# The first queries of an attention kernel loaded ahead of the values and transposed among the warm-up matmuls

## The chip, the cores and the metric

The kernel runs on one core of one Trainium2 chip. The metric is the device time of one execution in microseconds, the median of 13 runs: 168.59 us (168.45 to 169.01). A profile is one such execution, recorded by the hardware.

## The reference

Two stages follow each other. The first is attention in blocks with a learned sorting of the key and value blocks; the second is a maxout layer of two matmuls.

```python
for _ in range(5):                                  # P: 4 x 8 matrices of 8 x 8
    P = P - np.max(P, axis=-1, keepdims=True)
    P = np.exp(P)
    P = P / (np.sum(P, axis=-1, keepdims=True) + 1e-09)
    P = P / (np.sum(P, axis=-2, keepdims=True) + 1e-09)
k_sorted = np.einsum('bhij,bhjcd->bhicd', P, k_b)   # blocks of 96 tokens
v_sorted = np.einsum('bhij,bhjcd->bhicd', P, v_b)
scores = scale * np.matmul(q_b, k_sb.transpose(0, 1, 2, 4, 3))
attn = softmax(scores)                              # over the 96 tokens of the block
x = np.matmul(attn, v_sb)                           # then (3072 tokens, 512)
out = np.maximum(x @ w1, x @ w2) @ w_out            # 512 -> 1024 -> 512
```

There are 4 items (batch), 8 heads, 768 tokens, head size 64. All inputs come as float32 and are cast to bf16 while they are loaded.

## The kernel before, in words

The order of all instructions is written out by hand; no scheduler moves them. Each engine takes its own instructions in that order and waits on semaphores where it needs another engine's result. TensorE computes, ScalarE and VectorE bring results from PSUM to SBUF, GpSimd (POOL) issues all loads and SyncE (SP) the stores. PSUM is one ring of four buffers of 4 KB per partition (L62, tag `ps`): every product stage takes the next buffer, and waits until the last reader of that buffer is done.

The head of the kernel prepares the first item:

- POOL issues the loads in the order values 0 (three pieces, `load_v`, L169), the identity matrix, keys 0 (three pieces, L160), queries 0 (four pieces, one for each pair of heads, L143), then the expert weights (L189, L182). A later DMA that uses the semaphore of an earlier one waits until that one has landed.
- `sinkhorn` (L241) runs five times on the 32 x 64 tile `p_sb`: an exp on ScalarE (L242), then six short steps on VectorE (L248 to L255). The last writes `p_bf`. After the first two come mask steps on VectorE, after the third `selections`.
- `turn_v` (L219) reorders the values in SBUF. ScalarE does 18 columns after each of the third and the fourth sinkhorn step's VectorE part has been issued, and 20 and 24 after the fifth; VectorE does the last 16 of 96 after the masks. The turns stand between the exps in ScalarE's queue.
- `keep_streaming` (L77) multiplies zeros, so that TensorE is kept busy: 86 matmuls of 142 columns first, then two groups of six of 512 columns, each of which waits for a small VectorE fill that stands in the fourth and the fifth sinkhorn step (`late_zeros`, L85).
- `block_diagonals` (L317 to L335) makes from `p_bf` the two 128 x 64 matrices that sort keys and values.
- `sort_k` (L408, three groups) and `sort_v` (L429, four groups) follow, each evicted with a cast by the engine that the call names ("A" ScalarE, "D" VectorE). `q_transposes` (L383) turns one half of the queries, 24 transposes into one PSUM buffer, and evicts with one VectorE copy of 128 x 1536. The first half stands between the second and the third `sort_v`, the second half after the first two score groups.
- Scores (L498, exp L506), values (L525; reciprocal and product by VectorE, L536 and L542), transposes of x (L563) and the first expert products (L627) then alternate in a written order. Query half 0 serves head pairs 0 and 1, half 1 pairs 2 and 3; scores 2 need half 1. The x transposition 0 needs values 0 and 1, transposition 1 needs values 2 and 3; expert products (0, 2) need the first, (1, 3) the second.

After the head a loop over the four items issues expert and output products, and between them the attention steps of the next item (`first_tail` and so on). There `pick` gives an eviction to ScalarE or VectorE by counts of their load, which every earlier eviction has changed.

## Time and profile before

| | us |
|---|---|
| median of 13 runs | 168.59 |
| the profiled execution | 168.59 |
| its span, first to last instruction | 166.8 |
| TensorE matmul busy | 160.1 |
| ScalarE busy | 83.1 |
| VectorE busy | 79.3 |
| first product on `p_bf` starts | 11.53 |
| first key product starts | 12.71 |
| expert products (1, 3) start | 25.81 |

Times inside the span count from its start. A line of the timeline gives start, length, engine, line, operation, output and inputs, shape, count, and in brackets how long the engine stood idle before it and what ended that. A count over one merges neighbours of the same kind. A matmul line's length includes the drain of its last matmul, so it overlaps the line after it. The chain of waits goes back from the last instruction to whatever released it; its lines give start, length and what.

### The profile page before, as it was taken

The numbers are of one execution on the slowest core, as the hardware profiler recorded it, in microseconds if no ns is written. First come the engines' busy times: TensorE is split into PE (matmuls) and PEld (weight loads), VectorE is DVE, ScalarE is ACT, GpSimd is POOL, SyncE is SP. The second block draws the span as 40 slices with busy tenths as digits, with TensorE's granted clock in tenths as the row PEclk, the third lists the DMA queues.
The fourth block names the chain that finished last, engine by engine and source line by source line (L and its number), as shares of the span: only waits on it lengthen the run. The fifth ranks groups of instructions, "written<-read, shape, count | busy, mean of one in ns | idle before, by whom it ended". The sixth has DMA issues, their size and how long they took to land.

```text
span 166.8 us, 4555 instructions
## 1 busy us (share of the span) xinstructions
PE 160.1 (96%) x2011; PEld 96.7 (58%) x2011; DVE 79.3 (48%) x182; ACT 83.1 (50%) x101; POOL 29.6 (18%) x46
## 2 busy tenths in 40 slices
PE   7999899999999999999999999999999999999991
PEld 7948676766545555557655554575655545654451
DVE  5878885847483784535257874080642420000011
ACT  3587868674168627045752253467447206642010
POOL 7956586231022000000004120000000000000000
PEclk9999999999999999999999999999999999999999
DMA  3999999999999993659403999988025253000342
GB/s 54 191 203 196 198 207 206 212 201 216 212 210 210 216 230 77 173 111 199 106 0 61 148 232 182 188 223 110 2 51 173 47 177 126 0 0 0 126 154 103
DMA packets 30404, 23.90 MB, mean 143 GB/s; under 512 B 16752, under 2 KB 25200, under 8 KB 30384
## 3 DMA queue, kind: packets, MB, share of 16 engines
q0 software_dynamic: 11040, 13.37, 47.7%
q1 hardware_dynamic: 19200, 10.17, 25.9%
q8 instruction: 16, 0.26, 0.6%
q10 hardware_dynamic: 144, 0.07, 0.1%
q14 instruction: 4, 0.03, 0.1%
HBM read 26.75 MB, written 6.29 MB: 198 GB/s over the span
## 4 chain that ended last, share of the span: by engine, by line
PE 89%; DVE 4%; ACT 3%; issue 2%; ACTq 0%
PE out_ps L654 35%; PE h_ps L627 25%; PE fill_ps L82 6%; PE wc_ps L607 4%; PE k_ps L408 4%; PE o_ps L525 4%; PE s_ps L498 3%; PE tq_ps L383 2%; DVE x L542 1%; PE v_ps L473 1%; PE tw_ps L588 1%; ACT e L506 1%; DVE v_dc L227 1%; PE v_ps L429 1%; ACT xT L108 1%
## 5 line engine op out<-in xcount | busy, mean ns | idle before, releaser
L654 PE MATMUL out_ps<-wo_sb,g 128*128 128x512 bf16 (+2 forms) x200 | 48.3, 371 | 0.1
L627 PE MATMUL h_ps<-xT,w_sb 128*128 128x384 bf16 x256 | 44.4, 326 | 0.3 <-ACT xT L108 0.3
L627 PEld LDWEIGHTS <-w_sb 128*128 128x128 bf16 x256 | 24.2, 98 | 16.1 <-issue 0.4
L506 ACT ACTIVATE e<-s_ps 96x768 bf16<-96x768 f32 x32 | 24.2, 805 | 14.8 <-PE s_ps L498 14.8
L641 ACT ACTIVATE g<-h_ps 128x768 bf16<-128x768 f32 x27 | 21.9, 811 | 17.0 <-PE h_ps L627 16.9
L654 PEld LDWEIGHTS <-g 128*128 128x128 bf16 x200 | 17.1, 97 | 15.8
L654 PE MATMUL out_ps<-wc,xT 128*128 128x512 bf16 (+2 forms) x100 | 24.8, 370 | 0.0
L108 ACT COPY o<-out_ps 128x1024 f32<-128x1024 f32 x9 | 9.1, 1012 | 28.3 <-PE out_ps L654 25.7
L542 DVE TENSOR_TENSOR x<-o_ps,rs 96x512 bf16<-96x512 f32 x32 | 22.0, 687 | 1.1
L654 PEld LDWEIGHTS <-xT 128*128 128x128 bf16 x100 | 9.6, 97 | 11.2
L525 PEld LDWEIGHTS <-e 96*128 96x128 bf16 x256 | 11.5, 97 | 5.5
L689 DVE COPY o<-out_ps 128x512 f32<-128x512 f32 (+1 forms) x2 | 1.2, 625 | 27.6 <-PE out_ps L654 27.6
L536 DVE RECIPROCAL rs<-o_ps 96x8 f32<-96x8 f32 x32 | 6.4, 200 | 16.5 <-PE o_ps L525 16.5
L525 PE MATMUL o_ps<-v_sb,e 96*128 96x65 bf16 x256 | 12.7, 193 | 0.0
L110 DVE CAST v_sb<-v_ps 96x1024 bf16<-96x1024 f32 x8 | 9.7, 1217 | 5.4 <-PE v_ps L473 4.3
L643 DVE TENSOR_SCALAR g<-h_ps 128x768 bf16<-128x768 f32 x5 | 4.8, 955 | 12.1 <-PE h_ps L627 12.1
L110 DVE CAST kT<-k_ps 128x1024 bf16<-128x1024 f32 x6 | 7.2, 1221 | 6.0 <-PE k_ps L408 6.0
L108 ACT CAST v_sb<-v_ps 96x1024 bf16<-96x1024 f32 x8 | 8.0, 1008 | 3.1 <-PE v_ps L473 1.7
L160 POOL DMA_DIRECT2D v_raw<-in_k_dram x3 | 2.5, 825 | 38.4 <-DVE rs L536 38.3
L498 PE MATMUL s_ps<-qT,kT 64*128 64x96 bf16 x256 | 8.7, 204 | 0.5 <-DVE qT L110 0.4
L498 PEld LDWEIGHTS <-kT 64*128 64x128 bf16 x256 | 6.0, 94 | 5.4 <-issue 2.3
L82 PEld LDWEIGHTS <-fill 128*128 128x128 bf16 x91 | 8.0, 122 | 1.7 <-DVE fill L73 1.2
(85 smaller groups left out, 145.1 us busy)
## 6 DMA issues: line engine op xcount, KB each, us to landing
out_dram<-o SPq DMA_DIRECT2D x11, 512.0 KB, 3.0
v_raw<-in_v_dram POOLq DMA_DIRECT2D x8, 384.0 KB, 13.3
k_raw<-in_k_dram POOLq DMA_DIRECT2D x9, 256.0 KB, 10.0
w_sb<-in_moe_w_dram POOLq DMA_DIRECT2D x4, 256.0 KB, 9.5
w_sb<-in_moe_w_dram POOLq DMA_DIRECT2D x2, 512.0 KB, 11.2
wo_sb<-in_moe_w_out_dram POOLq DMA_DIRECT2D x2, 512.0 KB, 14.5
v_raw<-in_v_dram POOLq DMA_DIRECT2D x3, 256.0 KB, 4.6
q_raw<-in_q_dram POOLq DMA_DIRECT2D x4, 192.0 KB, 8.9
```

What stands on the lines that cost most here:

```text
L82: nc.tensor.matmul(ps[:, 0:w], w0, fill[:, 0:w], start=True, stop=True)
L108: nc.scalar.copy(out=out_ap, in_=in_ap)
L110: nc.vector.tensor_copy(out=out_ap, in_=in_ap)
L408: nc.tensor.matmul(ps[r0 : r0 + 64, m * 64 : (m + 1) * 64], kv[r0 : r0 + 64, t * 16 + m, :], bd_k[b][r0 : r0 + 64, :], start=True, stop=True,)
L498: nc.tensor.matmul(ps[:, h2 * 512 + ii * 128 : h2 * 512 + ii * 128 + BLK], kT[b][rows, (hp * 8 + i) * BLK : (hp * 8 + i) * BLK + 128], rhs ...
L506: nc.scalar.activation(out=e[:, 0 : 8 * BLK].rearrange("p (t c r) -> p t c r", t=8, r=R), in_=ps[0:BLK] .rearrange("p (t f) -> p t f", t=8 ...
L525: nc.tensor.matmul(ps[:, h2 * 512 + ii * 65 : h2 * 512 + (ii + 1) * 65], e[:, (h2 * 4 + ii) * BLK : (h2 * 4 + ii) * BLK + 128], v_sb[:, m0 ...
L542: nc.vector.tensor_tensor(out=x, in0=ov[:, :, :, 0:D], in1=rs.to_broadcast([BLK, 2, 4, D]), op=ALU.mult,)
L607: nc.tensor.matmul(ps[:, 0:512], w2T[:, fb, dmt * 128 : (dmt + 1) * 128], wo_sb[:, fb, :], start=(fb == 0), stop=(fb == NFB - 1),)
L627: nc.tensor.matmul(h_ps[t][:, m * 512 : m * 512 + TCH], w1_sb[:, hp, fb * 128 : (fb + 1) * 128], xT[:, b % 2, ch, hp % 2, hp // 2, :], sta ...
L641: nc.scalar.activation(out=g, in_=src, func=AF.Relu)
L654: nc.tensor.matmul(dst, g_tiles[b, ch, m // 2][:, m % 2, off : off + 128] if m < NFB else xT[:, b % 2, ch, hp % 2, hp // 2, off : off + 12 ...
```

## The change

Half of the first item's queries (pieces 0 and 1) is loaded before the values; the other half stays where it was. Its 24 transposes are issued after 50 zero matmuls of 175 columns and before 12 more, in place of 86 of 142 columns. Two ScalarE copies of 128 x 768 evict them, placed after the third sinkhorn step. The value turn loses its share there: ScalarE does 18, 20 and 20 columns, VectorE 20 and 18. The value evictions 2 and 3 change engines, and the order of values, scores and x transposes in the first item is altered, with one group of 512 zero columns less.

```diff
-    load_v(0, 3)
+    load_q(0, (0, 1))
     ident = const.tile([128, 128], BF16, tag="ident", name="ident")
     make_identity(nc, ident)
+    load_v(0, 3)
     load_k(0)
-    load_q(0, True)
+    load_q(0, (2, 3))
...
-        if b == 0 and half == 0:
-            nc.tensor.matmul(
-                ps[:, 0:128], fill[:, 0:128], ident, is_transpose=True, start=True, stop=True
-            )
...
+        def keep(hp0, hp1):
+            evac(
+                qT[b][:, half * 2 + hp0 : half * 2 + hp1].rearrange("p h r c -> p (h r c)"),
+                ps[:, hp0 * R * 128 : hp1 * R * 128],
+                (hp1 - hp0) * R * 128,
+                two_x=True,
+                eng=eng,
+            )
+
+        if later:
+            return keep
+        keep(0, 2)
...
-    keep_streaming(ps_f32("fill_ps"), 86 * 142, most=142)
+    keep_streaming(ps_f32("fill_ps"), 50 * 175, most=175)
+    keep_q = q_transposes(0, 0, "A", True)
+    keep_streaming(ps_f32("fill_ps"), 12 * 175, most=175)
     for it in range(5):
         sinkhorn(it)
         if it < 2:
             masks(it)
         if it == 2:
             selections(0)
+            keep_q(0, 1)
+            keep_q(1, 2)
+        if it == 3:
             turn_v(first, "A", 0, 18)
-        if it == 3:
-            turn_v(first, "A", 18, 36)
-    turn_v(first, "A", 36, 56)
-    turn_v(first, "A", 56, 80)
+    turn_v(first, "A", 18, 38)
+    turn_v(first, "A", 38, 58)
     block_diagonals([(0, 0), (1, 0)])
-    turn_v(first, "D", 80, 96)
+    turn_v(first, "D", 58, 78)
+    turn_v(first, "D", 78, 96)
...
     sort_v(0, 1, 0, "A")
-    q_transposes(0, 0, "D")
-    sort_v(0, 2, 0, "A")
-    sort_v(0, 3, 0, "D")
+    sort_v(0, 2, 0, "D")
+    sort_v(0, 3, 0, "A")
     SC[0]()
     SC[4]()
     q_transposes(0, 1, "D")
     SC[1]()
     VA[0]()
     SC[2]()
-    values(0, 1, 512)
+    VA[1]()
     SC[3]()
-    values(0, 2, 512)
+    VA[2]()
     x_transposes(0, 0, "A")
-    VA[3]()
-    VA[4]()
+    values(0, 3, 512)
     SC[5]()
     moe_h_products(0, 0, 0, (0, 2), 512)
     x_transposes(0, 1, "A")
+    VA[4]()
     SC[6]()
+    moe_h(0, 0, 0, "A", (1, 3))
     VA[5]()
-    moe_h(0, 0, 0, "A", (1, 3))
     SC[7]()
-    VA[6]()
     moe_h(0, 0, 1, "A")
     x_transposes(0, 2, "A")
+    VA[6]()
     w_difference(2)
+    w2T_ready = w2_transposes(0, "D")
     VA[7]()
-    w2T_ready = w2_transposes(0, "D")
     w_difference(3)
     w2T_ready()
```

## The prediction, made before the changed kernel was run

> **What bounds the kernel now.** I read the page first: its share of busy time, then the chain that ended last in order of time, then the timelines of TensorE, ScalarE and VectorE over the first 27 us, since every edit lies there.

> ```profile
> PE 160.1 (96%) x2011; PEld 96.7 (58%) x2011; DVE 79.3 (48%) x182; ACT 83.1 (50%) x101; POOL 29.6 (18%) x46
> ```

> TensorE is busy 96% of the span. In the windows after 27 us it is busy almost without a gap, so what counts is when that gapless stretch begins and how much TensorE work is still left then. The chain in order of time (start, length, what) tells where the head's time goes:

> ```profile
> 1.20 10.40 PE fill_ps L82 x98
> 11.59 0.17 PE pe L317 x2
> ...
> 12.71 1.71 PE k_ps L408 x96
> ...
> 18.98 0.97 DVE qT L110
> 19.95 0.05 issue
> 19.99 0.36 PE s_ps L498 x8
> ...
> 25.81 0.81 PE h_ps L627 x4
> ```

> Up to 11.5 us the chain is zero matmuls. That hides a second chain of about the same length: sinkhorn, which passes between ScalarE (exp) and VectorE. ScalarE's timeline from 5.98 us:

> ```profile
> 5.98 0.26 ACT L242 ACTIVATE p_sb<-p_sb 32x64 f32<-32x64 f32 x1 [1.65 <-DVE p_sb L255]
> 6.15 1.19 ACT L222 COPY v_dc<-v_raw 64x1152 bf16<-64x1152 bf16 x1
> 7.75 0.26 ACT L242 ACTIVATE p_sb<-p_sb 32x64 f32<-32x64 f32 x1 [0.42 <-DVE p_sb L255]
> ```

> The value turn starts right after the third exp and ends at 7.34; the fourth exp starts at 7.75, when VectorE has delivered. ScalarE has 0.4 us to spare per step, no more. The last sinkhorn step, `p_bf`, ends at 11.25 (VectorE's timeline: start 11.04, 0.21 long), and the first product on it starts at 11.53. So TensorE's zeros end some 0.24 us after sinkhorn does: sinkhorn has 0.24 us of slack, and any more delay of an exp delays everything.

> TensorE's and VectorE's lines of the part between:

> ```profile
> 1.20 7.81 PE L82 MATMUL fill_ps<-fill 128*128 128x142 bf16 x86 [1.20 <-DVE fill L73]
> 8.84 2.75 PE L82 MATMUL fill_ps<-fill,late 128*128 128x512 bf16 x12
> ...
> 15.55 0.86 PE L383 MATMUL tq_ps<-ident,q_raw 128*64 128x128 bf16 x24
> ```

> ```profile
> 12.71 0.70 DVE L227 COPY v_dc<-v_raw 64x512 uint32<-64x512 uint32 x1
> 13.95 1.22 DVE L110 CAST kT<-k_ps 128x1024 bf16<-128x1024 f32 x1 [0.54 <-PE k_ps L408]
> 15.09 1.21 DVE L110 CAST v_sb<-v_ps 96x1024 bf16<-96x1024 f32 x1
> 16.45 0.96 DVE L110 COPY qT<-tq_ps 128x1536 bf16<-128x1536 bf16 x1 [0.15 <-PE tq_ps L383]
> 17.48 1.22 DVE L110 CAST v_sb<-v_ps 96x1024 bf16<-96x1024 f32 x1
> 18.98 0.96 DVE L110 COPY qT<-tq_ps 128x1536 bf16<-128x1536 bf16 x1 [0.27 <-PE tq_ps L383]
> ```

> VectorE is nearly full from 12.4 to 19.94 us. That stretch is bound by VectorE together with the four PSUM buffers, not by TensorE.

> [...] the 86 zeros start at 1.20 and the next group at 8.84, 7.64 us; with 118.3 ns (cold) and 61.7 ns (warm) for 142 columns this gives 41 cold ones, a change at 6.07 us, and the windows count 10 matmuls from 5.20 to 6.10 and 18 from 6.10 to 7.00. [...] the trace has 0.80 for the copy of 128x768 bf16 at 22.70, and three exps of 0.81 in 2.21 us, a step of 0.70. I use the trace's.

> **The change, part by part.**

> *Query transposes among the zeros.* In the program as built the two ScalarE copies stand between the third and the fourth exp, and the first waits for the count of all 24 transposes. Queued behind it on ScalarE are the second copy, the fourth exp, the value turn, the fifth exp; VectorE's fourth sinkhorn step waits for that exp, TensorE's second late zeros for the end of that step, and everything after for `p_bf`. When can the copy start? The 50 zeros of 175 columns go ahead of the transposes. [...] From 1.20 to 6.07 us 33.4 are done; the other 16.6 take 1.25 us: 7.32 us. The transposes need the two query loads: these are now the first DMAs, issued at 1.24 and about 1.98 (0.74 us each on POOL). They carry 384 KB where the first value piece has 256 KB and landed at 1.24 + 4.1 = 5.34; at the 200 KB/us of the page's GB/s row that adds 0.65, so I estimate 6.0 to 6.4. They are in time. The 24 transposes took 0.90 us from their first start to the start of VectorE's cast (15.55 to 16.45): ScalarE starts at 7.32 + 0.90 = 8.22, with a little drain 8.25. Two copies: 0.80 + 0.70 = 1.50, end 9.75, with the usual overlap the fourth exp at 9.68 instead of 7.75: **+1.93 us**. From there to the end of `p_bf` nothing changes: 11.25 + 1.93 = 13.18, and a hand-over of 0.04 with a weight load of 0.03 gives the first product at 13.25 where it was 11.53: **+1.72 us**.

> *TensorE's own queue* costs nothing beside that: 7.32 + 0.85 for transposes + 12 x 75.4 ns = 9.1, six late zeros of 0.216 to 10.4, six more once VectorE's step releases them at about 11.4, end 12.8: covered by sinkhorn. Without that cover it would be 11.43 + 0.2, that is +0.2.

> *Values and keys land later.* 384 KB go ahead of them: +1.95 us. The last key piece landed at about 12.1 (next DMA behind it starts at 12.38), so about 14.1; its products, at 13.85 before, would have waited 0.3, but with +1.72 they come at 15.6. The value turns now begin at about 9.9 and the first value piece is there at about 7.3. Cost nothing. The weight loads keep their place by bytes; the third and fourth query piece also.

> *The sort stage, from 12.71 to the cast of the second query half at 19.94.* Gone from it: 24 transposes and a zero one on TensorE (about 0.95), one 0.96 cast on VectorE. New on VectorE: turns of 20 and 18 columns for one of 16, 0.70 x 38/16 = 1.66 instead of 0.70. The two cancel on VectorE. Its line, all shifted: turns start 14.43 and 15.23, key cast 15.94 (its products are ready at 15.67), value casts 17.08 and 18.22, the latter ends 19.44. The second half's transposes take over that cast's PSUM buffer (ring of four): 19.48, + 0.90 = 20.38, + 0.96 = 21.34 where it was 19.94. The stage gives back 1.72 - 1.40 = **0.32 us**. The bounds of this: nothing, if the longer turns come through in full, and 2.33 if all that goes came off the path: 0.95 of TensorE, 0.96 of VectorE and the waits of 0.15 and 0.27 before its two query casts. I take 0.32, since VectorE's line leaves no room for more.

> *New order of values and scores, one zero matmul fewer.* Scores 2 follow the cast, values 1 follow them, now without 512 zeros (0.23): x 1 ends at 22.10 + 1.40 - 0.23 = 23.27; its transposition and ScalarE's copy follow as before, 24.67. The first expert products wait for that copy: 24.97 (before 23.77). The second transposition needs values 3, now issued after the first: products at 24.03, x done at 25.37, before the products end at 25.62. So copy 26.16 to 26.97, products (1, 3) at 27.01 where they were 25.81: **+1.20 us**. But one group of values more is still to do from there (5, 6, 7 instead of 6, 7): **+0.24** (the chain's `o_ps` x8). From here TensorE is full. The planner then gives a few casts to other engines (one xT cast and the later query cast to VectorE); they have slack of over 1 us there: 0, or up to 0.2 either way.

> Sum: +1.72 - 0.32 - 0.20 + 0.24 = **+1.44 us**. The profiled execution took 168.59 us (span 166.8, 1.8 around it), the same as the median, so the forecast is 168.59 + 1.44 = **170.0**, about 0.9% slower.

> **The rivals.**
> 1. *The sort stage gives it all back (faster).* If all that goes comes off the path (2.33 instead of 0.32), the sum is +1.72 - 2.33 - 0.20 + 0.24 = -0.57: 168.0. For it: the stage's path passes both the transposes and their cast. Against it: the longer turns stand ahead of the key cast on VectorE. It decides at 1.76 given back: the stage would have to shrink from 7.23 to under 5.5 us.
> 2. [...] Then the zeros end at 5.7, the loads release the transposes at about 6.2, the copies end at 8.6 and the exp slips 0.8 instead of 1.93: +0.56 - 0.28 = +0.3, 168.9. Against it: 13 runs within 0.56 us[...].
> 3. *Queries land after 7.3*, by up to 1 us: 170.5 to 171. [...]
> 4. *The clock falls back.* TensorE now stands still for about 1.0 us before the last zeros and 0.5 after them, on top of the 0.8 at the masks that it has already. [...]

> **How the numbers follow.** Forecast 0.70 (169.4 to 170.6), rival 1 0.10, rival 2 and half-way cases within 0.2% 0.09, rivals 3 and 4 and the rest 0.11. 0.2% is 0.34 us, about what a measurement of this kernel tells from no change. Faster 0.11, same 0.09, slower 0.80. The range 168.8 to 171.0 takes in all but rival 1 and the top of 4.

> **What would show it.** Right: the fourth exp at 9.5 to 9.9 behind two ScalarE copies; idle ScalarE from 6.2 to 8.2; TensorE waiting twice before `pe`; `pe` at 13.1 to 13.4; the first key product near 14.4; products (1, 3) near 27.0. Wrong: the fourth exp before 8.5, or the second query cast ending before 20.0.

## The result, and the profile after

| | before | after |
|---|---|---|
| median, us | 168.59 (48 runs, 168.18 to 170.09) | 170.74 (11 runs, 170.18 to 171.07) |
| ratio of the times | | 1.0112, 95% interval 1.0096 to 1.0128 |
| profiled execution, us | 168.59 (span 166.8) | 170.40 (span 168.6) |
| first product on `p_bf` starts | 11.53 | 13.05 |
| first key product starts | 12.71 | 14.23 |
| expert products (1, 3) start | 25.81 | 26.12 |

The changed kernel is 1.1% slower. The forecast was 170.0 in a range of 168.8 to 171.0, so the time fell inside it and on the side given 0.80; the narrower 169.4 to 170.6, given 0.70, was just missed by the median. But the sum came out for partly wrong reasons, as the trace shows. The comparisons leave out single executions more than 1.5% above their kernel's fastest; the profiled executions of two experiments (the new order alone, the same count of zeros) are such, so from these two only waits are read, not their span.

ScalarE's timeline of the changed kernel shows what was expected: it stands idle for 1.90 us until TensorE's transposes are done, then makes two copies, and the fourth exp comes behind them.

```profile
5.96 0.26 ACT L245 ACTIVATE p_sb<-p_sb 32x64 f32<-32x64 f32 x1 [1.66 <-DVE p_sb L258]
8.12 1.50 ACT L108 COPY qT<-tq_ps 128x768 bf16<-128x768 bf16 x2 [1.90 <-PE tq_ps L382]
9.50 0.25 ACT L245 ACTIVATE p_sb<-p_sb 32x64 f32<-32x64 f32 x1
11.26 0.26 ACT L245 ACTIVATE p_sb<-p_sb 32x64 f32<-32x64 f32 x1 [0.43 <-DVE p_sb L258]
```

TensorE's timeline of the changed kernel, from the transposes to the expert products on weight piece 2:

```profile
7.21 0.86 PE L382 MATMUL tq_ps<-ident,q_raw 128*64 128x128 bf16 x24
...
11.36 1.47 PE L82 MATMUL fill_ps<-fill,late 128*128 128x512 bf16 x6 [0.97 <-DVE late L87]
13.05 0.20 PE L320 MATMUL pe<-p_bf,sel_v 32*128 32x64 bf16 x1 [0.22 <-DVE p_bf L258]
...
19.04 0.86 PE L382 MATMUL tq_ps<-ident,q_raw 128*64 128x128 bf16 x24 [0.62 <-DVE v_sb L110]
20.95 0.34 PE L503 MATMUL s_ps<-qT,kT 64*128 64x96 bf16 x8 [0.43 <-DVE qT L110]
21.23 0.42 PE L530 MATMUL o_ps<-v_sb,e 96*128 96x65 bf16 x8
...
26.12 0.81 PE L632 MATMUL h_ps<-xT,w_sb 128*128 128x384 bf16 x4 [0.37 <-ACT xT L108]
...
31.06 1.48 PE L632 MATMUL h_ps<-xT,w_sb 128*128 128x384 bf16 x8 [0.48 <-DVE w_sb L208]
```

Set beside the same groups of the kernel before, the delay is +1.52 at 13.05, +0.96 at the second half's transposes (19.04, before 18.08), +0.50 at values 1 (21.23, before 20.73), +0.31 at the expert products (1, 3). Four fifths of the delay of sinkhorn is given back within 13 us. Then it grows again: +1.20 at 31.06 (before 29.86), +1.44 near 58 us, +1.35 from 63 us on, +1.92 near 83, +1.81 at the end. VectorE's timeline tells why the products at 31.06 wait: the subtraction that makes the weight difference (L208) stands behind a normalization of x (L547), which waits for values 6. Those were moved behind the expert products.

```profile
14.23 1.36 DVE L230 COPY v_dc<-v_raw 64x640 uint32<-64x640 uint32 x2
15.52 1.21 DVE L110 CAST kT<-k_ps 128x1024 bf16<-128x1024 f32 x1
16.65 2.33 DVE L110 CAST v_sb<-v_ps 96x1024 bf16<-96x1024 f32 x2
19.94 0.96 DVE L110 COPY qT<-tq_ps 128x1536 bf16<-128x1536 bf16 x1 [0.95 <-PE tq_ps L382]
...
29.48 0.20 DVE L541 RECIPROCAL rs<-o_ps 96x8 f32<-96x8 f32 x1 [1.34 <-PE o_ps L530]
29.72 0.69 DVE L547 TENSOR_TENSOR x<-o_ps,rs 96x512 bf16<-96x512 f32 x1
30.32 0.68 DVE L208 TENSOR_TENSOR w_sb<-w_sb 128x1024 bf16<-128x1024 bf16 x1
```

The rows of TensorE's waits in the changed kernel (total, times, longest) name two that the kernel before does not have behind its head:

```profile
PE s_ps L503 <- DMA qT<-q_pair: 0.5, 1, 0.5
PE h_ps L632 <- DVE w_sb L208: 0.5, 1, 0.5
```

The first is in the chain of the changed kernel as well. The queries of the third item are turned by a DMA transposition, and scores wait for its end:

```profile
73.58 2.24 PE h_ps L632 x14
75.82 6.37 DMA qT<-q_pair
82.19 0.14 issue
82.32 0.52 PE s_ps L503 x16
```

In the DMA records of the changed kernel a packet of 16 KB of the queue that the profile calls "instruction" starts at 80.32, and the transposition's packets stop for 0.61 us from 80.65 on, after some 2040 of their 3072. In the kernel before, such packets start at 75.0 and 81.4. Its transposition's packets stop too, for 0.62 us from 77.55 on, but after some 500; the first transposition lands 5.5 us after its issue there, and 6.4 us in the changed kernel. So a stop alone does not tell the two kernels apart.

### The profile page after: what moved, and what is told of

It is laid out like the page before. It is cut to its first block, busy times and chain, and to the rows that moved or that the text cites. A ratio compares the mean times of both kernels' runs of the same rounds, so it can differ in the third digit from the quotient of the medians.

```text
span 168.6 us, 4500 instructions
## 1 busy us (share of the span) xinstructions
PE 159.2 (94%) x1985; PEld 95.8 (57%) x1985; DVE 79.7 (47%) x183; ACT 81.9 (49%) x101; POOL 29.9 (18%) x46
## 4 chain that ended last, share of the span: by engine, by line
PE 78%; DVE 10%; DMA 4%; ACT 4%; issue 3%; ACTq 0%; DVEq 0%
PE out_ps L659 33%; PE h_ps L632 23%; PE wc_ps L612 4%; DMA qT<-q_pair 4%; PE o_ps L530 4%; PE fill_ps L82 4%; PE s_ps L503 4%; DVE v_sb L110 3%; ACT e L511 2%; PE k_ps L413 2%; PE tq_ps L382 2%; DVE v_dc L230 2%; PE tx_ps L568 1%; ACT qT L108 1%; DVE kT L110 1%
## 5 line engine op out<-in xcount | busy, mean ns | idle before, releaser
L646 ACT ACTIVATE g<-h_ps 128x768 bf16<-128x768 f32 x26 | 21.1, 811 | 18.4 <-PE h_ps L632 18.4
L108 ACT COPY o<-out_ps 128x1024 f32<-128x1024 f32 x10 | 10.1, 1012 | 28.5 <-PE out_ps L659 25.9
L547 DVE TENSOR_TENSOR x<-o_ps,rs 96x512 bf16<-96x512 f32 x32 | 22.0, 687 | 1.1
L648 DVE TENSOR_SCALAR g<-h_ps 128x768 bf16<-128x768 f32 x6 | 5.7, 958 | 12.0 <-PE h_ps L632 12.0
L110 DVE CAST v_sb<-v_ps 96x1024 bf16<-96x1024 f32 x8 | 9.6, 1213 | 3.5 <-PE v_ps L478 2.4
L110 DVE CAST kT<-k_ps 128x1024 bf16<-128x1024 f32 x6 | 7.1, 1217 | 5.0 <-PE k_ps L413 5.0
L171 POOL DMA_DIRECT2D v_raw<-in_v_dram x11 | 5.8, 535 | 14.1 <-DVE v_dc L230 9.7
## 6 DMA issues: line engine op xcount, KB each, us to landing
w_sb<-in_moe_w_dram POOLq DMA_DIRECT2D x4, 256.0 KB, 10.4
w_sb<-in_moe_w_dram POOLq DMA_DIRECT2D x2, 512.0 KB, 11.4
```

The costliest lines, as they stand in the source:

```text
L108: nc.scalar.copy(out=out_ap, in_=in_ap)
L110: nc.vector.tensor_copy(out=out_ap, in_=in_ap)
L547: nc.vector.tensor_tensor(out=x, in0=ov[:, :, :, 0:D], in1=rs.to_broadcast([BLK, 2, 4, D]), op=ALU.mult,)
L646: nc.scalar.activation(out=g, in_=src, func=AF.Relu)
```

## The experiments

The edits are made to the changed kernel unless the kernel before is named. Each was timed beside the kernel before, whose median there was 168.67 us (runs 1 to 4), 168.88 (5 to 8) and 168.70 (9 to 12). The ratios are taken as above and differ a little from those of the medians.

**1. The copies behind the fourth exp.**

```diff
         if it == 2:
             selections(0)
-            keep_q(0, 1)
-            keep_q(1, 2)
         if it == 3:
-            turn_v(first, "A", 0, 18)
+            keep_q(0, 1)
+            keep_q(1, 2)
+    turn_v(first, "A", 0, 18)
```

> The changed kernel with its two ScalarE copies of the turned queries behind the fourth exp instead of ahead of it; the first value turn goes behind the fifth exp. My theory (the copies hold up the exp, 1.75 us): the fourth exp starts at 7.7 to 7.8 again, the fifth near 9.6, the first product on p_bf near 11.7, and the time falls by 1.0 to 1.3 us to 169.4 to 169.7. Rival (the keys are the next wait: their third piece landed at about 15.2 in the changed kernel, and its products would now be due at about 14.0): the exps come back all the same, but TensorE waits for the third key piece, and the time falls by 0.1 to 0.5 only. Second rival (head does not matter): no change.

Measured: 170.06 (169.96 to 172.68), ratio 1.0085 (1.0072 to 1.0099). The fourth exp is back at 7.92 and the first product on `p_bf` at 12.00 instead of 13.05; yet only 0.7 us came through by the medians, 0.5 by the ratios (1.0112 and 1.0085). The rival in the expectation was right in kind. A row of this kernel's waits shows what came next:

```profile
PE k_ps L413 <- DMA k_raw<-in_k_dram: 0.6, 1, 0.6
```

With the exps early, the third group of key products waits for keys that land late, at about 14.9, behind 384 KB of queries. The delay of the exp and that of the keys lie side by side, and taking one away leaves the other.

**2. Values 6 ahead again.**

```diff
     SC[7]()
+    VA[6]()
     moe_h(0, 0, 1, "A")
     x_transposes(0, 2, "A")
-    VA[6]()
     w_difference(2)
```

> The changed kernel with values group 6 issued ahead of the second expert products, as in the kernel before, instead of behind the third x transposition. Theory (the third weight difference is queued behind x of group 6 on VectorE and the expert products of column piece 2 wait for it): that difference starts near 28.8 instead of 30.32, the 0.5 to 0.6 us wait of those products is gone, and the time falls by 0.5 to 0.6. Rival (the wait only moves to the next evictions): within 0.2 of the changed kernel.

Measured: 170.29 (170.17 to 170.56), ratio 1.0100 (1.0087 to 1.0114), 0.45 less than the changed kernel by the medians and 0.2 by the ratios, whose intervals overlap. The wait for `w_sb` is gone from the rows; the wait for the transposition stays at 0.6.

**3. The planner's load counts as before.**

```diff
+    load["A"] -= 2 * (200 + 768) / 1.2
+    load["D"] += (130 + 768) / 0.96
     for b in range(1, B):
```

> The changed kernel, with the planner's two load counters set after the head to what the kernel before had there, so that it hands out later evictions as before. Theory (the other assignments cost 0.25 us near 58 us and shift what the query transposes by DMA wait for near 76 to 82 us): the time falls by 0.25 to 0.7. Rival (the later waits come from the shifted position of the transfers or from chance in their landing): within 0.2 of the changed kernel.

Measured: 170.74 (170.05 to 171.09), ratio 1.0119 (1.0100 to 1.0138): no different from the changed kernel. In its trace a step of 0.25 near 58 us has gone (against the changed kernel it stands at +0.56 up to there and at +0.31 behind it), but 0.1 of it is lost again by 64 us (+0.41). The medians do not show the rest, and the interval of some 0.3 us leaves it open.

**4. The new order alone**, in the kernel before (the order of values, scores and x transposes of the change's last part, nothing else).

```diff
-    values(0, 1, 512)
+    VA[1]()
     SC[3]()
-    values(0, 2, 512)
+    VA[2]()
     x_transposes(0, 0, "A")
-    VA[3]()
-    VA[4]()
+    values(0, 3, 512)
...
```

> The kernel before with only the changed order of values, x transposes and expert products (and one group of 512 zero columns less); loads, query transposes, copies and turns as before. Theory: earlier expert products by 0.2 to 0.6, then 0.24 of values still to do and about 0.6 of waiting for the third weight difference: between 0 and 0.6 us slower than the kernel before. Rival (the new order is a gain which the head hides): 0.2 to 0.6 faster than the kernel before.

Measured: 170.32 (169.39 to 172.14), ratio 1.0086 (1.0057 to 1.0115). Its executions differ by what clock TensorE was granted: the three with a mean of 0.997 or more took 169.39, 169.58 and 169.91. So the order by itself costs 0.7 to 1.2 us at full clock, which is more than the 0 to 0.6 expected, and more than the +0.04 (-0.20 and +0.24) that the prediction put on its parts. TensorE's timeline early in this kernel:

```profile
19.75 0.34 PE L498 MATMUL s_ps<-qT,kT 64*128 64x96 bf16 x8 [0.42 <-DVE qT L110]
20.50 0.42 PE L525 MATMUL o_ps<-v_sb,e 96*128 96x65 bf16 x8 [0.40 <-PE s_ps L498]
```

The zeros ahead of values 1 are left out, but the values start at 20.50, where the kernel before starts those zeros, and after a wait that no engine explains (the scores named were TensorE's own). Why 20.50 again is taken up below.

**5. The same count of matmuls.** The changed kernel has 26 TensorE matmuls fewer than the kernel before: by the pages 3970 instructions and 15 packets of the queue "instruction", where the kernel before has 4022 and 16. Its 16 KB packets come at other moments (80.32, where the kernel before has 75.0 and 81.4). Here the 50 zeros become 76 narrower ones with the same columns.

```diff
-    keep_streaming(ps_f32("fill_ps"), 50 * 175, most=175)
+    keep_streaming(ps_f32("fill_ps"), 50 * 175, most=116)
```

> The changed kernel with its 50 leading zero matmuls of 175 columns cut into 76 of at most 116 (the same 8750 columns), so that TensorE has as many instructions as in the kernel before, 26 pairs more than in the changed one. Theory (TensorE's instructions come in 16 KB pieces by DMA, one per 256 of them; with 26 pairs less the piece at 80.3 us falls amid the second query transposition by DMA, which then stands still for 0.6 us): that piece falls elsewhere, the scores near 80 to 82 us no longer wait for the DMA, and the time falls by 0.4 to 0.6. Rival (the transposition is late because it was issued later or for another transfer): no change, the 0.5 us wait stays.

Measured: 172.44 (169.82 to 173.07), ratio 1.0149 (1.0091 to 1.0208). The wait for the transposition is gone, as expected, but a new one stands in the rows of this kernel:

```profile
PE s_ps L503 <- issue: 0.5, 1, 0.5
```

TensorE waits for nothing that the profile shows. So the time did not fall by the 0.4 to 0.6 expected. In five of six executions the clock also fell (mean 0.98 to 0.99); the one at full clock took 169.82.

**6. All mended**: the edits of runs 1, 2, 3 and 5 together.

> The changed kernel with four things undone: copies behind the fourth exp, values group 6 ahead, planner loads as before, count of TensorE instructions as before. If the four losses are what they seem and add (0.7, 0.6, 0.25, 0.5), the changed kernel's 170.7 comes to 168.6 to 169.0, no faster than the kernel before, since TensorE still waits about 0.6 us for the third key piece. Rival: they overlap, and it stays above 169.3; or the early queries then gain something, under 168.4.

Measured: 170.42 (169.50 to 171.43), ratio 1.0093 (1.0057 to 1.0128). The four of its eight executions at a clock of 0.999 or more took 169.50 to 169.94, the others (0.98 to 0.99) 170.90 to 171.43. Even these stay above the 169.3 that the rival named: the four losses do not add. Waits of 0.5 for the third keys and of 0.5 by "issue" remain.

**7. The kernel before with fewer zeros**: 60 of 204 columns instead of 86 of 142, the columns the same.

```diff
-    keep_streaming(ps_f32("fill_ps"), 86 * 142, most=142)
+    keep_streaming(ps_f32("fill_ps"), 86 * 142, most=204)
```

> The kernel before with its 86 zero matmuls of 142 columns as 60 of at most 204 (the same 12212 columns), thus 26 instruction pairs less; nothing else differs. Theory of the instruction pieces: the pieces that were at 75.0 and 81.4 us move by about 2 us, one falls amid the query transpositions by DMA (74.5 to 80.9 us), and the kernel gets slower by 0.3 to 0.7, with TensorE waiting for the transposition near 80 us. Rival (the count of instructions is of no matter): within 0.15 of the kernel before[...].

Measured: 173.24 (172.27 to 175.11), ratio 1.0241 (1.0200 to 1.0282). None of the work behind the zeros was touched, but TensorE's timeline has a hole of 3.2 us in the middle of the query transposes:

```profile
15.29 0.69 PE L383 MATMUL tq_ps<-ident,q_raw 128*64 128x128 bf16 x18
19.20 0.53 PE L383 MATMUL tq_ps<-ident,q_raw 128*64 128x128 bf16 x6 [3.21 <-issue]
```

The first 16 KB instruction packet of this run starts at 16.94, where it starts at 11.76 in the kernel before. This hole was not foreseen. The wait that was foreseen came too: this kernel's rows have 0.4 us of scores waiting for the DMA transposition. The clock was also at half from 17.88 to 24.71.

**8. Only the head of the change**: the loads, the transposes, the copies and the turns as changed; the order, the planner's counts and the number of matmuls as before.

```diff
-    keep_streaming(ps_f32("fill_ps"), 50 * 175, most=175)
+    keep_streaming(ps_f32("fill_ps"), 50 * 175, most=117)
...
-    VA[1]()
+    values(0, 1, 512)
...
+    load["A"] -= 2 * (200 + 768) / 1.2
+    load["D"] += (130 + 768) / 0.96
```

> Only the head of the change (loads, transposes among the zeros, ScalarE copies, turns, value evictions), with the order of values of the kernel before, its planner loads and its count of TensorE instructions. It has the steps of the prediction up to the second query cast alone. By the prediction: fourth exp +1.75 to 1.93, first product on p_bf +1.5 to 1.7, second query cast ends +1.0 to +1.4, and all of that at the end: 169.6 to 170.0. Rival (the head costs little, the order of values and what follows made most of the loss): within 0.5 of the kernel before.

Measured: 170.53 (170.13 to 172.55), ratio 1.0126 (1.0080 to 1.0172). That is above both the theory and the rival. In its profile the clock rises at 4.33 us, 1.3 earlier than in that of the changed kernel. (The rise is where the record of the granted clock starts. In the kernel before that is 6.10, and the step between the starts of its zeros falls there from 118.3 to 61.7 ns; in the changed kernel it is 5.63, and the step falls from 146.7 to 75.8 ns.) So the zeros end sooner, the fourth exp starts at 8.92, and the second half's transposes come only 0.39 late. Then TensorE's timeline has another hole that no engine explains:

```profile
20.38 0.34 PE L503 MATMUL s_ps<-qT,kT 64*128 64x96 bf16 x8 [0.42 <-DVE qT L110]
21.93 0.61 PE L82 MATMUL o_ps<-fill 128*128 128x512 bf16 x1 [1.20 <-issue]
```

**What these holes are.** I counted TensorE's instructions (a weight load and a matmul each count one) up to every such restart, and set the restarts (the start of the weight load) beside the 16 KB packets of the queue "instruction":

| kernel | packet starts | TensorE goes on | after | at its instruction |
|---|---|---|---|---|
| before with fewer zeros (7) | 16.94 | 19.20 | 2.26 | 446 |
| count from the late zeros (10) | 13.28 | 15.58 | 2.30 | 445 |
| count from the late zeros (10) | 19.38 | 21.77 | 2.39 | 701 |
| only the head (8) | 19.52 | 21.92 | 2.40 | 702 |
| same count (5) | 20.02 | 22.45 | 2.43 | 702 |
| all mended (6) | 19.20 | 21.57 | 2.37 | 702 |
| new order alone (4) | 18.07 | 20.50 | 2.43 | 702 |
| before, split cast (12) | 18.26 | 20.49 | 2.23 | 701 |
| **before** | 18.10 | 20.50 | 2.40 | 702 |

At quite different times TensorE stops ahead of the same two instructions (to within one), 256 apart, and goes on 2.2 to 2.4 us after a packet starts. By the page of the kernel before, 16 packets stand beside 4022 instructions of TensorE, 251 for each. So I read the holes as waits for the next instructions. Meanwhile the loads moved about 200 GB/s (201 in run 7, 202 in run 5, from 9 to 24 us); that they are the reason for the holes is not shown. Where TensorE did not stop at instruction 446, the second packet starts 3.0 to 3.6 us after it passed there (4.3 in run 8); with the 2.2 to 2.4 us of the table, my estimate for the 256 instructions from there is 5.2 to 6.0 us at least. In the kernel before they take from 15.06 to 20.50. **The kernel before itself is held there**, for 0.17 us by its own row:

```profile
20.50 0.39 PE L82 MATMUL o_ps<-fill 128*128 128x512 bf16 x1 [0.17 <-PE s_ps L498]
```

**9. Both late waits of the changed kernel removed**: run 2's edit, and the transposition issued earlier.

```diff
-        20: [VA[4]],
+        20: [VA[4], lambda: q_transposes(2, 0), lambda: q_transposes(2, 1)],
...
-        0: [lambda: q_transposes(2, 0), lambda: q_transposes(2, 1)],
```

> The changed kernel with two edits far behind its head: values 6 issued ahead of the second expert products (as in the run that took the wait for the weight difference away), and the two query transpositions of the third item issued before, not behind, the last two x transpositions of the second item and the output store that waits on SyncE. Theory (each of the two waits, 0.45 measured and 0.5 read from the wait rows, is time on TensorE's gapless stretch): 170.74 - 0.45 - 0.5 = 169.8, no row of scores waiting for the DMA transposition. Rival (the stall of the transposition is only handed on to the x transpositions, which now stand behind it): 170.3, with a wait for xT from DMA. Rival (the time at 80 us was made good later anyway): 170.3 with no such wait.

Measured: 169.80 (169.42 to 172.71), ratio 1.0064 (1.0049 to 1.0078): the theory's number. The view of the tile `q_pair` gives the first issue at 70.2 instead of 75.8 and the landing after 3.9 to 4.6 us, instead of up to 6.4; it lists nobody who waits, and no wait for an x transposition takes the place.

```profile
L372 SPq DMA_TRANSPOSE qT<-q_pair x4: 1489/1692/2114, 70.2 to 110.5; - x4
...
DMA to landing us min/median/max: 3.9/4.3/4.6
```

**10. The count restored from the late zeros**, in run 7's kernel: the two groups of six zeros of 512 columns become two of nineteen of 162.

```diff
-            keep_streaming(ps_f32("fill_ps"), 3072, it)
+            keep_streaming(ps_f32("fill_ps"), 3072, it, most=162)
```

> The kernel before with 60 leading zero matmuls of 204 columns (that alone took 173.24 and stood still 3.2 us at the 449th TensorE instruction), and the late zeros cut into 38 of 162 columns instead of 12 of 512: the same columns at the same places, 26 matmuls more, so the count of 98 of the kernel before. Theory ([...]): no stall, 168.4 to 169.2. Rival (wider or faster zeros, or the clock that rose earlier, cause it): the stall of about 3 us stays, 172 to 174.

Measured: 170.70 (169.74 to 172.46), ratio 1.0110 (1.0078 to 1.0142), against 173.24 in run 7. The hole of 3.2 us has shrunk to 0.56, and the packet comes at 13.28 instead of 16.94; a second hole opens 256 instructions later. TensorE's timeline of this kernel:

```profile
14.12 0.90 PE L429 MATMUL v_ps<-bd,v_dc 64*128 64x64 bf16 x25
15.58 0.38 PE L429 MATMUL v_ps<-bd,v_dc 64*128 64x64 bf16 x7 [0.56 <-issue]
...
20.49 0.34 PE L498 MATMUL s_ps<-qT,kT 64*128 64x96 bf16 x8 [0.42 <-DVE qT L110]
21.78 0.39 PE L82 MATMUL o_ps<-fill 128*128 128x512 bf16 x1 [0.94 <-PE s_ps L498]
```

The width of the zeros is ruled out as the cause of the 3.2 us: the 60 wide ones are still there. That the count alone decides is not confirmed either, since the time did not come back to 168.6. What differs from the kernel before is when the instructions are passed: the 128th at 8.45 us here, at 7.42 there.

**11. The copies, values 6 and the transposition together**: the edits of runs 1 and 9.

> The changed kernel with the two late edits and with the two ScalarE copies of the queries behind the fourth exp, as in the run that moved only these. Theory (the parts add): 170.74 - 0.68 - 0.45 - 0.5 = 169.1, still slower than 168.6, by the wait for the third keys (0.5 to 0.6) and the group of values left over. Rival (with more taken away the next wait takes over): 169.6 to 169.8, no faster than the kernel with the two late edits alone.

Measured: 169.87 (169.30 to 173.95), ratio 1.0056 (1.0038 to 1.0075). The rival was nearer than the theory: by the ratios it is only 0.1 us beyond run 9, and the intervals overlap. Its first product on `p_bf` starts at 11.47, earlier than in the kernel before, and its waits show where that goes:

```profile
PE k_ps L413 <- DMA k_raw<-in_k_dram: 0.8, 1, 0.8
```

Here it is the second keys that TensorE waits for (at 14.18); the third group waits a little again (the 64 products from there take 1.53 us, where 64 take 1.20 in run 1).

**12. A version that might beat both**: the kernel before, its zeros 138 columns wide (the count kept), and the cast of its second query half in two pieces.

```diff
-    keep_streaming(ps_f32("fill_ps"), 86 * 142, most=142)
+    keep_streaming(ps_f32("fill_ps"), 86 * 138, most=138)
...
-        evac(
-            qT[b][:, half * 2 : half * 2 + 2].rearrange("p h r c -> p (h r c)"),
+        for hp0, hp1 in [(0, 1), (1, 2)] if b == 0 and half == 1 else [(0, 2)]:
+            evac(
+                qT[b][:, half * 2 + hp0 : half * 2 + hp1].rearrange("p h r c -> p (h r c)"),
...
```

> The kernel before with two small edits that the study points to: 86 leading zeros of 138 instead of 142 columns (the count kept; sinkhorn had about 0.2 us of slack to them), and the cast of the second query half in two pieces, as the changed kernel does with the first half, so that scores 2 need only the first piece. Theory: -0.2 from the zeros, scores 2 at 19.3 instead of 19.99, of which VectorE, next in line with its normalizations, lets 0.2 through: 168.2. Rival (the clock or the next wait takes it back): 168.5 to 168.8. [...]

Measured: 168.70 (168.44 to 169.74, 14 runs), ratio 1.0000 (0.9982 to 1.0019). TensorE's timeline of this kernel:

```profile
19.41 0.34 PE L499 MATMUL s_ps<-qT,kT 64*128 64x96 bf16 x8
20.50 0.39 PE L82 MATMUL o_ps<-fill 128*128 128x512 bf16 x1 [0.74 <-DVE rs L537]
```

The first product on `p_bf` starts at 11.36 instead of 11.53. That need not be the edit's doing, since the clock rose at 5.09 instead of 6.10 in this profile, and in run 4, with unchanged zeros and a rise at 5.61, this product started at 11.29. Scores 2 start at 19.41 instead of 19.99, 0.58 earlier. Then the zeros start at 20.50, as in the kernel before. The reciprocal named as releaser ended at 19.92, long before, so it is not what TensorE waited for; by the reading above its 701st instruction was, which came 2.23 us after the packet at 18.26. The whole gain is taken there. No version that was run beats the kernel before.

## Why the prediction was right, and where it was not

| step | forecast | measured |
|---|---|---|
| fourth exp | 9.68 (+1.93) | 9.50 (+1.75) |
| first product on `p_bf` | 13.25 (+1.72) | 13.05 (+1.52) |
| given back up to the second query cast | 0.32 | 0.56 |
| expert products (1, 3) | 27.01 (+1.20) | 26.12 (+0.31) |
| the group of values left over | +0.24 | +0.26 |
| behind that | 0, up to 0.2 either way | +1.24 |
| sum | +1.44 | +1.81 between the profiles, +2.15 between the medians |

**The head was right.** The copy that heads ScalarE's queue holds the exp behind it, as the prediction read it from the order (the copies end at 9.62, the exp starts at 9.50, overlapped). That 33.4 of the 50 zeros are done by 6.07 us, and 75.4 ns for each one behind that, were the author's estimates; in the changed kernel's trace zeros of 175 columns start every 146.7 ns up to 5.57 us and every 75.8 ns behind it. The 0.2 less is a clock that rose earlier, at 5.63 instead of 6.10, so that the 50 zeros ended at 7.2. TensorE's two waits in the head came, 0.97 and 0.22, where the prediction had about 1.0 and 0.5. From the end of `p_bf` to the first product the chain has 0.05 us, where the prediction put an estimate of 0.07. In the profile the queries landed at 4.8 and 5.8, ahead of rival 3, and the mean granted clock of the changed kernel was 1.0 in all its executions, so rival 4 did not come. But the reason given against rival 2, an earlier rise of the clock (its 5.7 us was the author's estimate), does not hold: in spite of thirteen like times the clock rises anywhere from 4.23 to 7.19 us over the profiles of this study. With the copies ahead of the fourth exp, this exp follows it: 8.92 for a rise at 4.33 (run 8), 9.50 for 5.63, 10.25 for 7.19 (run 5). The kernel before hides this, because sinkhorn covers its zeros: with its head unchanged but for the width of the zeros, the first product on `p_bf` started at 11.29 for a rise at 4.23 (run 7) as for one at 5.61 (run 4). So rival 2 is the early end of a spread, and the head's cost is no fixed number. Nor is rival 4 ruled out for kernels like this one: the clock fell to half in the profiles of runs 4 to 8, as shown at the end.

**"The stage gives back 0.32" was too small**, and the terms that were mis-sized can be named. The turns were scaled with their columns (0.70 x 38/16 = 1.66); the two take 1.28 (14.23 to the next cast at 15.52), since 640 and 576 elements take 0.71 and 0.72 where 512 took 0.70, and the second starts 0.63 after the first. With `p_bf` 0.20 earlier than forecast, everything to the second cast is 0.42 to 0.46 earlier. The given-back part is 1.52 - 0.96 = 0.56.

**The order of values was sized at -0.20 and gave -0.65** (from +0.96 to +0.31). The zeros left out give 0.23, as forecast. The kernel before also stands at its 702nd instruction until 20.50; the changed kernel has 26 matmuls fewer between the key products and there, so its 702nd instruction lies further on in its work, past values 1, and it is not held there: it passes at 22.68, 2.8 us after the packet at 19.90. Values 1 have only +0.50 of the +0.96 left at 21.23: 0.23 by the zeros, and 0.23 that fits the 0.17 of that wait and its hand-over. The rest of the give-back, to +0.31, is in the steps from 21 to 24 us; I did not separate it by a run. Run 4 does show that the order is no gain where the head is as before: there it was held at 20.50 all the same, and later by the wait for `w_sb` (0.5).

**"From here TensorE is full" failed.** It took the chain of the kernel before for that of the changed one. Two waits came up. Moving values 6 put a VectorE normalization ahead of the weight difference: +0.63 by the shifts, 0.45 by run 2. The prediction followed the moved groups on TensorE alone and not the queue of VectorE that they feed.

The other is the wait for the transposition: 0.5 by the row, 0.57 by the shifts, and 170.29 - 169.80 = 0.49 by runs 2 and 9. It goes with the 26 matmuls fewer: it stands in the five profiles that have them and issue the transposition behind the output store (the changed kernel, runs 1, 2, 3 and 7), and in none of the seven with all of them or all but one. In these five an instruction packet starts 0.32 to 0.33 us ahead of the stop in the transposition's packets. But a stop of 0.58 to 0.87 us stands in the other seven profiles too, 0.8 to 2.7 us behind a packet, and only runs 9 and 11, which issue the transposition ahead of the store, have none. How the packet brings the wait about is therefore open; that the two waits cost time is shown by run 9.

Run 9 explains 0.94 of the 2.15 by the medians, 0.81 by the ratios (1.0112 and 1.0064). The split between the two waits is 0.45 and 0.49 by the medians, 0.2 and 0.6 by the ratios. The traces side with the ratios: against the changed kernel the shift from the expert products (1, 3) to 70 us falls by 0.28 both in run 2 (+0.30 to +0.02) and in run 9 (+0.23 to -0.05), and by 0.57 at the transposition in run 9. So of the 0.63 less than half comes back when values 6 stand where they were. The planner's part, 0.15 net by the trace and within the prediction's "up to 0.2", could not be told from nothing in run 3. These make up what lies behind the head: 0.63 + 0.15 + 0.57, less 0.11 that is made good by the end.

**"Values and keys land later. Cost nothing" held only by its cover.** In the changed kernel the third keys land at about 15.2 (POOL's weight issue that waits for them starts at 15.49) instead of the 14.1 that I estimated, 3.1 later than before and not 1.95; why is open. Their products start at 15.25, just as they are in. (In the kernel before these start at 13.72, not at the 13.85 that the prediction read.) In run 1 the cover is gone and the wait for the third keys is 0.6, in run 11 0.8 is waited for the second keys already, and not the 0.3 that the prediction put on it. Freeing the exp is therefore worth 0.68 by the medians in run 1 (0.46 by the ratios) and 0.1 by the ratios in run 11.

So the forecast was near the result in part by luck, because two errors met: 0.9 us too much up to the expert products (1, 3) (0.2 in the head, 0.24 in the sort stage, 0.45 in the order of values), 1.2 too little behind them.

## What to carry to other kernels

When a group is moved on one engine, follow every instruction that it feeds on the other engines, and look at what stands behind those in their queues: here the cost was not on the engine whose order was changed. When time is freed at the start of a stage, look for the next thing that arrives by a clock of its own (in run 1 a load, 0.6 us; in run 12, as I read it, the next instructions, 0.74) before counting it as gain. A change in the number of instructions is a change too: here 26 matmuls fewer in the head went with a wait of 0.5 us at 82 us. Run 7 changed nothing but the count and the width of the zeros, and stood still for 3.2 us.

## What the runs showed of the hardware

```profile
14.47:17.88 3.41, 1.52 (x45) 1.00 1.42 197
17.88:21.30 3.42, 2.10 (x39) 0.50 1.40 199
21.30:24.71 3.41, 3.34 (x63) 0.50 1.24 207
24.71:28.12 3.41, 3.11 (x67) 1.00 1.24 206
```

In the profiles of runs 4 to 8 the window before the fall was busy for 2.20, 2.22, 2.40, 1.52 and 1.83 of 3.41 us; but windows with 2.23 (run 5, from 10.60) and 2.04 (run 11, from 11.58) were not followed by a fall. Busy time alone does not decide it, and what does stays open.
